# A planner that takes the longest-free buffer or PSUM bank instead of the lowest-numbered one, and a later due time for one transpose

## The chip, the core and the metric

The kernel runs on one core of one Trainium2 chip. A core has five engines with their own instruction queues: TensorE (PE, matrix multiplies and transposes into the eight PSUM banks), VectorE (DVE), ScalarE (ACT), GpSimd (POOL) and SyncE (SP, which here only issues DMAs). Each engine runs its queue in program order and waits on semaphores for the others. The metric is device time in microseconds, from the launch of the program to its end; lower is better.

## What is computed

Inputs are q, k, v of shape 2 x 8 x 768 x 64 (batch, heads, positions, head size) and four weight matrices. The reference is three steps:

```
state = gamma[head] * state + outer(k[t], v[t])      # per head, t = 0..767, gamma = 1 - 2**(-5-head)
y[t]  = 1/sqrt(64) * q[t] @ state                    # retention, a linear attention with decay
x  = softplus(y @ w_in)  @ w_out                     # y as 1536 x 512; w_in 512 x 2048, w_out 2048 x 512
out = hardswish(x @ w2_in) @ w2_out                  # hardswish(h) = h * clip(h + 3, 0, 6) / 6
```

The weights arrive as 64-bit floats and are read as pairs of 32-bit words.

## The kernel before

**Three kinds of work share the engines.** (1) Retention: 12 units, one for each batch and each chunk of 128 positions, in `attend(u)`. A unit loads k, q and v; transposes k and q on PE into PSUM; ACT copies kT out and DVE multiplies q by a scaling table into qT; PE computes scores; DVE masks them into `pt`; PE computes the state's increment (`product`: k with vs, the scaled v), the inner part (`inner`: pt with vs) and the carried part (`carry`: qT with the state `st`); ACT and DVE write the result as a high and a low part, `x_hi` and `x_lo`. (2) Weights: 64 tiles, each fetched as 64-bit words into `raw`, turned into float32 in `cv` by two ACT and three DVE instructions, and split into a high and a low part in `w` (the low part by DVE or by an adding DMA from POOL). (3) Two GEMM layers, `gemm1` and `gemm2`, 12 matmuls of 128 x 512 per step (high x high, high x low, low x high), 96 steps of `gemm1` and 96 of `gemm2`, with softplus or hardswish on ACT and DVE between them. The first four units of retention must be done before the first `gemm1`; the other eight are woven between GEMM steps.

**What sets the order.** The class `Plan` is a list scheduler that runs while the kernel is built. Each piece of work is a task with an engine, an estimated cost, the tasks it follows, a due time, and the slots that it takes and gives. `run` keeps an estimated clock for each engine, looks at the first 80 tasks of each, takes among those that can start within `NEAR` of the first (0.5 for PE) the one with the lowest due time, and issues its instructions at once. The order of those picks is the program order of every engine. The times in the planner are estimates made at build time; the chip only sees the order and which slot each task got.

**Slots.** A pool (`raw0`, `cv0`, `w`, `e`, `g`, `hi`, `lo`, `kT0`, `qT0`, `st`, ..., and `bank` for the eight PSUM banks) is a list of the estimated times from which each slot is free. `places` picks slots. It is called twice: without `at`, to learn when a task could start, and with `at`, the chosen start, to take slots. With `at` every slot free by then counted as equally free, so `sorted(..., key=(time, i))` took the lowest number and, for banks, `min` took the first group in the list of `bank_groups`. For units 0 to 3 that list is the pairs 2-3, 4-5, 6-7, 0-1 (or the single banks of these in that order); for later units only 2 and 3; `gemm1` alternates in 0 and 1, `gemm2` has 4 to 7. A slot taken again makes the first instruction that writes it wait, on the chip, for the last one that used it.

**The start of the program.** PE first runs 16 idle transposes, then `wide_turned`: four transposes that turn the scaling table (spread by DVE into an `e` tile) into PSUM under the key `tqP`. ACT copies that into `tq_sb`. Then come unit 0's transposes of k (`kP`) and of q (`qP`), 4 each. With the lowest number taken, `tqP`, `kP` and `qP` all sat in bank 2, one after another.

Of the kernel before, what the change touches and what calls it, by code (L numbers as in the profile page):

```python
# [22 lines left out]
class Plan:  # L23
# [37 lines left out]

    def places(self, pool, keys, at=None):

        times = {i: x if at is None else max(x, at) for i, x in enumerate(self.pools[pool]) if x is not None}
        if pool in self.groups:
            ok = [g for g in self.groups[pool](keys) if all(i in times for i in g)]
            return min(ok, key=lambda g: max(times[i] for i in g), default=None)
        return sorted(times, key=lambda i: (times[i], i))[:len(keys)] if len(times) >= len(keys) else None

    def run(self, log=None):  # L70
        free = {"PE": 0.0, "DVE": 0.0, "ACT": 0.0, "POOL": 0.0, "SP": 1.2}
        line = {"SP": 0.0, "POOL": 0.0}
        todo = {e: sorted((t for t in self.tasks if t.eng == e), key=lambda t: (t.due, t.n)) for e in free}
        left = {k: len(v) for k, v in self.users.items()}
        for _ in self.tasks:
            best = None
            for e, ts in todo.items():
                found = []
                for t in ts[:80]:
                    if any(a.done is None for a in t.after):  # L80
                        continue
                    at = max([free[e], t.hold] + [a.done + (self.LAG[a.eng] if a.eng != e else 0.0) for a in t.after])
                    for pool in {p for p, _ in t.take}:
                        ok = self.places(pool, [k for p, k in t.take if p == pool])
                        if ok is None:
                            break
                        at = max(at, max(self.pools[pool][i] for i in ok))
                    else:
                        found.append((at, t))
                if not found:  # L90
                    continue
                first = min(a for a, _ in found)
                at, t = min(((a, t) for a, t in found if a <= first + self.NEAR[e]), key=lambda x: (x[1].due, x[1].n))
                if best is None or at < best[0]:
                    best = at, t
            if best is None:
                raise RuntimeError("the plan is stuck: " + str([(e, ts[0].n, ts[0].take) for e, ts in todo.items() if ts]))
            at, t = best
            for pool in {p for p, _ in t.take}:
                keys = [k for p, k in t.take if p == pool]  # L100
                for key, i in zip(keys, self.places(pool, keys, at)):
                    self.pools[pool][i] = None
                    self.slot[key] = pool, i
            end = free[t.eng] = at + t.cost
            if t.load:
                other = "SP" if t.eng == "POOL" else "POOL"
                begin = max(line[t.eng], end + 1.2)
                shared = max(0.0, min(t.load, line[other] - begin))
                line[t.eng] = begin + t.load + shared
                line[other] += shared  # L110
                end = line[t.eng] + 0.5
            t.done = end
            for k in t.give:
                left[k] -= 1
                if not left[k]:
                    pool, i = self.slot[k]
                    self.pools[pool][i] = max(u.done for u in self.users[k])
            todo[t.eng].remove(t)
            if log is not None:
                log.append((at, end, t))  # L120
            t.fn()
# [7 lines left out]
def kernel(ctx, tc, q, k, v, w1_in, w1_out, w2_in, w2_out, table, out):  # L129
    nc = Plan(tc)  # L130
# [102 lines left out]
    due, t = {}, 5.0  # L233
# [158 lines left out]
    def bank(key):  # L392
        return at_slot(key).rearrange("p (n t) -> p n t", n=NP)
# [3 lines left out]
    def attend(u):  # L397
        b, i = divmod(u, NCH)
# [11 lines left out]
        def own(n):  # L410
            return [(f"{n}{ph}", (n, u))]
# [12 lines left out]
        if u < START:  # L424
            at = [begin + 10 * u, begin + 10 * u + 1, begin + 10 * u + 3]
        else:
            at = [d["Tk"] - 9.0, d["Tk"] - 8.5, d["Tk"] - 8.0]
# [4 lines left out]
        if u == 0:  # L432
            ready["t"] = nc.add("SP", 0.45, lambda: nc.sync.dma_start(out=tables, in_=table), [], begin - 1, load=0.1)
            t = nc.add("DVE", 0.62, spread_out, [ready["t"]], begin, take=[("e", "wide")])
            t = nc.add("PE", 0.46, wide_turned, [t], 0.0, take=[("bank", ("tqP", 0))], give=["wide"])
            ready["q"] = nc.add("ACT", ACP, lambda: nc.scalar.activation(tq_sb, bank(("tqP", 0)), AF.Copy), [t], begin, give=[("tqP", 0)])

        def turned(n):
            def go():
                for p in range(NP):  # L440
# [6 lines left out]
                  take=own("kT"), give=[("kP", u)])  # L447
# [29 lines left out]
        def middle():  # L477
            if first:
                nc.vector.tensor_copy(at_slot(mid[1]), sub(ds, 0))
            else:  # L480
# [3 lines left out]
                  give=ds + ([] if first else [("end", u - 1)]))  # L484
# [21 lines left out]
        def carry():  # L506
            for j in range(int(first), 2):
                w = at_slot(mid[1] if j else ("end", u - 1))
                for p in range(NP):
# [7 lines left out]
                 give=[mid[1], ("qT", u)] + ([] if first else [("end", u - 1)]))  # L517
# [10 lines left out]
    for u in range(NU):  # L528
        attend(u)
# [140 lines left out]
```

## Time and profile before

| | us |
|---|---|
| Median of 3 runs (lowest, highest) | 603.46 (602.60, 604.37) |
| Profiled execution, whole | 602.95 |
| its span, first to last instruction | 601.2 |
| around the span (602.95 - 601.2) | 1.75 |
| PE busy, of the span | 586.3 |
| PE not busy (601.2 - 586.3) | 14.9 |
| DVE busy, ACT busy | 326.4, 305.5 |

The profile is one execution. A row of the timeline gives the start and the length of an instruction or a run of like instructions, and in brackets how long its engine was idle before it and which engine's instruction released it. On PE a run of matmuls reads "start, length, output<-inputs, shape, count"; `ident,k` are the transposes of k, `qT,kT` the scores, `vs,k` the product, `pt,vs` the inner part, `qT,st` the carried part, `x_hi,w` a `gemm1`. The 64 x 64 matmuls show twice as many records as the program has instructions. A row of the windows view gives each engine's busy time within a stretch, then PEclk, the mean granted clock of TensorE as a share of full speed (its two levels are 1.2 and 2.4 GHz, 0.50 and 1.00).

### The profile page before, as it was taken

To read this page: it belongs to the slowest core of one execution; us is meant where nothing else is said; L and a number is where in the kernel's file an instruction comes from. 1 tells how busy PE (TensorE), PEld (TensorE's weight loads), DVE (VectorE), ACT (ScalarE), POOL (GpSimd) and SP (SyncE) were. 2 spreads that over 40 slices of the span, in tenths; PEclk is the share of its full clock that TensorE was granted. 3 is DMA by queue.
4 is the path that set the end of the run, shared out by engine and by line. 5 is a ranking of instruction groups with operands and counts; after the bars stand their busy time and mean duration, and the time that the engine had idled before them with its cause. 6 is when DMAs were issued, how large, how long until landed. Compare 5 with 4: busy or idle time off the path is not lost.

```text
span 601.2 us, 9628 instructions
## 1 busy us (share of the span) xinstructions
PE 586.3 (98%) x3895; PEld 479.1 (80%) x3895; DVE 326.4 (54%) x573; ACT 305.5 (51%) x515; POOL 40.3 (7%) x53
## 2 busy tenths in 40 slices
PE   7799999999999999999999999999999999999997
PEld 6678777878777788888888787888888888888886
DVE  3989999986544433566677876622422222412223
ACT  2469898895323333577789888622222222222220
POOL 0001111010000000011122222100000000000000
PEclk8789999999999999999999999999999999999999
DMA  9969887763111200065779988410100000100001
GB/s 198 243 159 228 223 219 191 203 148 71 41 31 37 71 1 0 1 151 130 179 181 225 224 207 200 98 19 0 71 0 1 1 1 0 71 0 1 1 0 70
DMA packets 67500, 58.56 MB, mean 97 GB/s; under 512 B 39552, under 2 KB 56192, under 8 KB 67456
## 3 DMA queue, kind: packets, MB, share of 16 engines
q1 hardware_dynamic: 60976, 46.15, 27.5%
q0 software_dynamic: 6480, 11.80, 11.3%
q8 instruction: 30, 0.49, 0.3%
q14 instruction: 14, 0.11, 0.1%
HBM read 43.00 MB, written 3.15 MB: 77 GB/s over the span
## 4 chain that ended last, share of the span: by engine, by line
PE 85%; DVE 4%; DMA 4%; ACT 4%; issue 1%; POOL 0%; DVEq 0%; SPq 0%; ACTq 0%; POOLq 0%
PE banks L42 85%; DMA raw<-in_moe_w_out_dram 4%; DVE cv L42 2%; ACT raw L42 1%; ACT w L42 1%; ACT cv L42 1%; ACT g L42 0%; ACT hi L42 0%; ACT e L42 0%; DVE raw L42 0%; DMA out_dram<-e 0%; DVE qT L42 0%; DVE g L42 0%; DVE pt L42 0%; DVE st L42 0%
## 5 line engine op out<-in xcount | busy, mean ns | idle before, releaser
L42 PE MATMUL banks<-x_hi,w 128*128 128x512 f32 x768 | 254.1, 393 | 2.0 <-DVE g L42 1.5
L42 PEld LDWEIGHTS banks<-x_hi,w 128*128 128x128 f32 x768 | 144.2, 188 | 34.0 <-DVE g L42 2.5
L42 PE MATMUL banks<-x_lo,w 128*128 128x512 f32 x384 | 149.6, 390 | 0.0
L42 PE MATMUL banks<-hi,w 128*128 128x512 f32 x384 | 127.8, 395 | 0.0
L42 PE MATMUL banks<-w,hi 128*128 128x512 f32 (+1 forms) x386 | 118.3, 388 | 0.0
L42 ACT ACTIVATE e<-banks,three 128x512 f32<-128x512 f32 x48 | 33.0, 686 | 128.2 <-PE banks L42 120.7
L42 DVE SCALAR_TENSOR_TENSOR g<-e,banks 128x512 f32<-128x512 f32 x48 | 33.0, 688 | 115.5 <-ACT e L42 115.1
L42 DVE TENSOR_TENSOR lo<-g,hi 128x512 fp32r<-128x512 f32 x96 | 66.1, 690 | 48.7 <-ACT hi L42 45.6
L42 DVE SCALAR_TENSOR_TENSOR cv<-raw,cv 128x512 uint32<-128x512 uint32 x128 | 87.5, 689 | 8.1 <-ACT cv L42 5.5
L42 ACT ACTIVATE hi<-g 128x512 fp32r<-128x512 f32 x96 | 60.5, 630 | 51.9 <-DVE g L42 36.3
L42 PEld LDWEIGHTS banks<-hi,w 128*128 128x128 f32 x384 | 72.1, 188 | 15.6
L42 PEld LDWEIGHTS banks<-w,hi 128*128 128x128 f32 x386 | 72.4, 188 | 14.9
L42 PEld LDWEIGHTS banks<-x_lo,w 128*128 128x128 f32 x384 | 72.1, 188 | 14.3
L42 PE MATMUL banks<-w,lo 128*128 128x512 f32 (+1 forms) x193 | 74.9, 388 | 0.0
L42 PE MATMUL banks<-lo,w 128*128 128x512 f32 x192 | 74.9, 390 | 0.0
L42 ACT ACTIVATE w<-cv 128x512 fp32r<-128x512 f32 x109 | 65.5, 624 | 8.0 <-DVE cv L42 7.6
L42 POOL DMA_DIRECT2D w<-cv x45 | 39.2, 872 | 349.4 <-ACT w L42 203.6
L42 ACT ACTIVATE g<-banks 128x512 f32<-128x512 f32 x48 | 28.6, 595 | 53.6 <-PE banks L42 51.1
L42 ACT ACTIVATE cv<-raw,half 128x512 uint32<-128x512 uint32 x64 | 48.2, 758 | 0.0
L42 ACT ACTIVATE raw<-raw 128x512 f32<-128x512 f32 x64 | 42.8, 668 | 3.6 <-DMA raw<-in_moe_w_out_dram 3.4
L42 PEld LDWEIGHTS banks<-w,lo 128*128 128x128 f32 x193 | 36.2, 188 | 7.5
L42 PEld LDWEIGHTS banks<-lo,w 128*128 128x128 f32 x192 | 36.1, 188 | 7.0
(58 smaller groups left out, 325.2 us busy)
## 6 DMA issues: line engine op xcount, KB each, us to landing
raw<-in_moe_w_in_dram SPq DMA_DIRECT2D x32, 512.0 KB, 4.1
raw<-in_moe_w_out_dram SPq DMA_DIRECT2D x32, 512.0 KB, 3.6
w<-cv POOLq DMA_DIRECT2D x45, 256.0 KB, 4.6
out_dram<-e SPq DMA_DIRECT2D x11, 256.0 KB, 2.0
q<-in_q_dram SPq DMA_DIRECT2D x8, 256.0 KB, 5.2
v<-in_v_dram SPq DMA_DIRECT2D x8, 256.0 KB, 5.4
k<-in_k_dram SPq DMA_DIRECT2D x7, 256.0 KB, 4.8
raw<-in_k_dram SPq DMA_DIRECT2D x4, 256.0 KB, 3.1
```

Of the source, the lines that this page charges most:

```text
L42: return self.plan.tc.keep_in_program_order(getattr(self.engine, op)(*args, **kwargs))
```

## The change

`places` keeps, for each free slot, the pair (time from which the task could have it, time since which it is free). Where several slots are free by `at`, the first entries are equal and the second decides: the one longest free is taken, in every pool and for bank groups alike. In `run` the start of a candidate is now the maximum over the slots' free times as before, written without the pair. The due time of `wide_turned` goes from 0.0 to 5.2, between unit 0's k (due 5.0) and q (5.46).

```diff
     def places(self, pool, keys, at=None):
 
-        times = {i: x if at is None else max(x, at) for i, x in enumerate(self.pools[pool]) if x is not None}
+        free = {i: x for i, x in enumerate(self.pools[pool]) if x is not None}
+        times = {i: (x if at is None else max(x, at), x) for i, x in free.items()}
         if pool in self.groups:
             ok = [g for g in self.groups[pool](keys) if all(i in times for i in g)]
             return min(ok, key=lambda g: max(times[i] for i in g), default=None)
@@ run
-                        at = max(at, max(self.pools[pool][i] for i in ok))
+                        at = max([at] + [self.pools[pool][i] for i in ok])
@@ attend, unit 0
-            t = nc.add("PE", 0.46, wide_turned, [t], 0.0, take=[("bank", ("tqP", 0))], give=["wide"])
+            t = nc.add("PE", 0.46, wide_turned, [t], 5.2, take=[("bank", ("tqP", 0))], give=["wide"])
```

The program order, first place: PE at the start of the program, from the turned scaling table (`ident,e`) to unit 0's scores (`qT0,kT0`). Rows with a minus are of before, with a plus of the changed kernel; the brackets name the semaphores waited on (`Activation` is ACT, `DMAHW` a load).

```order
 L42 MATMUL banks_65<-ident_139,e_0_103 128x128 x3
-L42 MATMUL banks_65<-ident_139,k0_0_123 128x128 [waits DMAHW1_49,Activation_49]
+L42 MATMUL banks_65<-ident_139,k0_0_123 128x128 [waits DMAHW1_49]
 L42 MATMUL banks_65<-ident_139,k0_0_123 128x128
 L42 MATMUL banks_65<-ident_139,k0_0_123 128x128 [waits DMAHW2_49]
-L42 MATMUL banks_65<-ident_139,q0_0_120 128x128 [waits DMAHW3_49,Activation_49]
+L42 MATMUL banks_65<-ident_139,q0_0_120 128x128 [waits DMAHW3_49]
 L42 MATMUL banks_65<-ident_139,q0_0_120 128x128 x3
-L42 MATMUL banks_65<-qT0_0_130,kT0_0_129 64x64 [waits DVE_49]
+L42 MATMUL banks_65<-qT0_0_130,kT0_0_129 64x64 [waits DVE_49,Activation_49]
```

The order of the rows is unchanged: the table's transposes still stand ahead of k's. What moved is the waits: k and q no longer wait for ACT, since the three take banks 2, 3 and 4; the scores now name ACT themselves, for kT. With the new due time alone the program is that of before row for row on all five engines, and with the new `places` alone it is the changed one.

Second place: PE from unit 3's transposes of k to unit 4's transposes of q, the last retention work but one ahead of the first `gemm1`. `k0_0` and the first `pt` are unit 3's, `k0_1` and `q0_1` unit 4's. First the kernel before, then the changed one.

```order
L42 MATMUL banks_65<-ident_139,k0_0_123 128x128 [waits DMAHW0_49,DVE_49]
L42 MATMUL banks_65<-vs0_0_132,k0_0_123 64x64 [waits DVE_49]
L42 MATMUL banks_65<-qT0_0_130,kT0_0_129 64x64 [waits Activation_49]
L42 MATMUL banks_65<-pt0_0_134,vs0_0_132 64x64 [waits DVE_49]
L42 MATMUL banks_65<-ident_139,k0_1_124 128x128 [waits DMAHW1_49,DVE_49]
L42 MATMUL banks_65<-ident_139,q0_1_121 128x128 [waits DMAHW2_49]
```

```order
L42 MATMUL banks_65<-ident_139,k0_0_123 128x128 [waits DMAHW0_49]
L42 MATMUL banks_65<-vs0_1_133,k0_0_123 64x64 [waits DVE_49]
L42 MATMUL banks_65<-qT0_1_131,kT0_0_129 64x64 [waits Activation_49]
L42 MATMUL banks_65<-ident_139,k0_1_124 128x128 [waits DMAHW1_49,DVE_49]
L42 MATMUL banks_65<-pt0_1_135,vs0_1_133 64x64 [waits DVE_49]
L42 MATMUL banks_65<-ident_139,q0_1_121 128x128 [waits DMAHW2_49]
```

Unit 4's transposes of k moved ahead of unit 3's inner part, and unit 3's transposes of k lost their wait for DVE.

Third place: PE among the GEMM steps, around the transposes of unit 5 (`k_0`, `q_0` before; `k_2`, `q_2` now). `x_hi_66,w_83` ends a `gemm1`, `hi_...,w_85` is a `gemm2`. First before, then changed.

```order
L42 MATMUL banks<-x_hi_66,w_83 128x512
L42 MATMUL banks<-hi_107,w_85 128x512
...
L42 MATMUL banks<-ident,k_0_123 128x128 x4
L42 MATMUL banks<-ident,q_0_120 128x128 x4
L42 MATMUL banks<-x_hi_66,w_84 128x512
...
L42 MATMUL banks<-qT_0_130,kT_0_129 64x64 x16
```

```order
L42 MATMUL banks<-x_hi_66,w_83 128x512
L42 MATMUL banks<-ident,k_2_125 128x128 x4
L42 MATMUL banks<-ident,q_2_122 128x128 x4
L42 MATMUL banks<-hi_108,w_85 128x512
...
L42 MATMUL banks<-qT_1_131,kT_0_129 64x64 x16
L42 MATMUL banks<-x_hi_66,w_84 128x512
```

From here to the end of unit 7 every retention piece stands one GEMM step earlier in PE's queue; DVE's and ACT's queues shift with it between their weight and softplus instructions. Behind that the orders of before and now are the same on every engine but for slot numbers.

## Rows read from the trace of the kernel before

**Rows 1.** Page, part 1: engine, busy us, share of the span, instructions

```profile
PE 586.3 (98%) x3895; PEld 479.1 (80%) x3895; DVE 326.4 (54%) x573; ACT 305.5 (51%) x515; POOL 40.3 (7%) x53
```

**Rows 2.** Windows: stretch, its us, busy us (instructions) of five engines, PEclk, DMA share, GB/s

```profile
6.50:10.00 3.50, 1.78 (x36) 1.31 (x40) 1.22 (x2) 0.72 (x2) 0.00 (x0) 0.99 1.26 222
10.00:13.40 3.40, 3.40 (x85) 2.83 (x78) 2.04 (x5) 0.60 (x1) 0.00 (x0) 0.51 1.32 221
13.40:23.60 10.20, 7.91 (x278) 6.73 (x280) 9.13 (x21) 5.10 (x9) 0.00 (x0) 1.00 1.02 262
23.60:33.80 10.20, 8.07 (x133) 6.58 (x130) 8.86 (x17) 3.84 (x8) 0.00 (x0) 0.50 0.59 161
33.80:37.00 3.20, 2.37 (x96) 2.12 (x93) 3.04 (x6) 2.78 (x5) 0.00 (x0) 1.00 1.24 291
```

**Rows 3.** Timeline of PE, 0 to 38 us

```profile
4.92 1.06 PE L42 MATMUL banks<-ident,e 128*128 128x128 f32 x4
6.67 0.66 PE L42 MATMUL banks<-ident,k 128*128 128x128 f32 x4 [0.69 <-ACT tq_sb L42]
8.02 0.66 PE L42 MATMUL banks<-ident,q 128*128 128x128 f32 x4 [0.69 <-ACT kT L42]
9.53 0.84 PE L42 MATMUL banks<-qT,kT 64*64 64x64 f32 x32 [0.85 <-DVE qT L42]
10.14 1.12 PE L42 MATMUL banks<-vs,k 64*64 64x64 f32 x32
...
13.30 0.66 PE L42 MATMUL banks<-ident,q 128*128 128x128 f32 x4
...
15.34 0.69 PE L42 MATMUL banks<-vs,k 64*64 64x64 f32 x32
...
17.33 0.66 PE L42 MATMUL banks<-ident,q 128*128 128x128 f32 x4
...
21.38 0.69 PE L42 MATMUL banks<-pt,vs 64*64 64x64 f32 x32 [1.24 <-DVE st L42]
...
24.10 1.11 PE L42 MATMUL banks<-ident,q 128*128 128x128 f32 x4
...
30.38 1.13 PE L42 MATMUL banks<-pt,vs 64*64 64x64 f32 x32 [1.29 <-DVE pt L42]
31.44 1.11 PE L42 MATMUL banks<-ident,k 128*128 128x128 f32 x4
32.34 1.06 PE L42 MATMUL banks<-ident,q 128*128 128x128 f32 x4
...
36.61 0.50 PE L42 MATMUL banks<-x_hi,w 128*128 128x512 f32 x1
```

**Rows 4.** Windows: one unit's stretch; the GEMM steps beside the weights

```profile
13.95:18.05 4.10, 3.78 (x123) 3.05 (x124) 3.78 (x8) 1.19 (x2) 0.00 (x0) 1.00 1.10 346
40.00:122.00 82.00, 81.53 (x730) 64.52 (x729) 77.06 (x148) 70.35 (x123) 8.83 (x10) 1.00 0.79 209
```

**Rows 5.** Timeline of PE, 100 to 125 us

```profile
121.33 0.50 PE L42 MATMUL banks<-x_hi,w 128*128 128x512 f32 x1 [0.47 <-ACT g L42]
```

**Rows 6.** Timeline of SP: issues of q and v of unit 0, q of unit 3

```profile
2.18 0.51 SPq L42 DMA_DIRECT2D q<-in_q_dram  x1
2.74 0.58 SPq L42 DMA_DIRECT2D v<-in_v_dram  x1
...
12.62 0.49 SPq L42 DMA_DIRECT2D q<-in_q_dram  x1
```

**Rows 7.** DMA issues from 1 to 3.3 us: KB each, median us to landing

```profile
q<-in_q_dram SPq DMA_DIRECT2D x1, 256.0 KB, 3.4
v<-in_v_dram SPq DMA_DIRECT2D x1, 256.0 KB, 4.1
```

**Rows 8.** Timeline of DVE, 0 to 38 us

```profile
33.44 0.69 DVE L42 TENSOR_TENSOR qT<-banks,tq_sb 128x512 f32<-128x512 f32 x1 [1.11 <-PE banks L42]
```

**Rows 9.** DMA issues from 12.6 to 22.7 us

```profile
q<-in_q_dram SPq DMA_DIRECT2D x2, 256.0 KB, 6.7
```

## The prediction

> **What bounds the kernel now.** I read the page first: PE is busy 586.3 of 601.2 us [rows 1], and nearly all of that is GEMM steps, which the change neither adds nor removes. So only PE's 14.9 idle us and its clock can move. Then the windows view, to see where they lie [rows 2]. From 6.5 to 37 us the five stretches last 30.5 us with PE busy 1.78 + 3.40 + 7.91 + 8.07 + 2.37 = 23.53: 6.97 idle us, nearly half of all. In two of these stretches PE runs at the lower clock, 10.0 to 13.4 (0.51) and 23.6 to 33.8 (0.50). Then PE's timeline of the start [rows 3], whose brackets name who ends each idle piece. From 40 to 122 us PE is busy 81.53 of 82.00 [rows 4]; the 0.47 left is one wait for ACT at 121.33 [rows 5]. DVE is busy 77.06 of those 82, 94%. So the start is a chain PE-ACT-PE-DVE-PE; from 13.4 on DVE carries it (9.13 and 8.86 of 10.2 busy [rows 2]); behind the first GEMM step at 36.61 PE is the bound and DVE close behind it.
>
> **The due time.** It removes, adds and moves nothing: with it alone every engine's order is that of before, since the table is ready so much ahead of k's load that the planner picks it first either way. Price 0. All that follows is the choice of slots.
>
> **Unit 0: two bank waits go.** Before, the table's transposes (4.92, 1.06 long, to 5.98), k's and q's share a bank: k starts 0.69 late, released by the copy to tq_sb, q 0.69 late, released by the copy to kT; the scores start 0.85 behind q's end (8.68 to 9.53), which is qT's multiply [rows 3]. With three banks k and q follow at once, if loaded: q is issued at 2.18 and v at 2.74 [rows 6] and land 3.4 and 4.1 later [rows 7], at 5.6 and 6.8; k is issued ahead of q. Four transposes take 0.66 here, but the table's took 1.06, the pace of the lower clock (1.06 and 1.11 stand again at 32.34 and 31.44, where PEclk is 0.50). The clock rose somewhere between 5.98 and 6.67, so k now falls across the rise: I take the mean, 0.86, for k and 0.66 for q. Then q ends at 5.98 + 0.86 + 0.66 = 7.50 and the scores start 0.85 later, 8.35 instead of 9.53: 1.2 gained. Bounds: both slow, 5.98 + 2.12 + 0.85 = 8.95, 0.6; both fast, 8.15, 1.4. The scores' new wait for ACT costs nothing: kT is ready 0.69 behind k's end, at 7.5, ahead of qT, and only the product stands behind the scores, which needs vs, made on DVE behind qT as before.
>
> **The clock behind it.** Ahead of the slow stretch at 10.0 PE was idle 3.50 - 1.78 = 1.72 us; in 33.8 to 37.0 it was idle 0.83 and the clock stayed at 1.00 [rows 2]. Without the two waits what is left in front is the 0.85, like the second case, so I expect the clock to stay up through 10.0 to 13.4. Worth: product, k, inner part up to the next q take 10.14 to 13.30, 3.16 us, at 0.51, and 15.34 to 17.33, 1.99, at 1.00: 1.17 at most. DVE has 2.04 us of its own in that stretch, which then fill it, so I take 0.9, between 0 (the clock falls all the same) and 1.2.
>
> **Units 2 and 3: waits that cost nothing.** The inner part at 21.38 waited 1.24 for DVE's state additions, which free its bank pair; it now has an older pair and waits only for its mask. Unit 3's k likewise no longer waits for the bank that its q left. I count both at 0: DVE is full there, and what PE does next waits for DVE's queue anyway. If DVE had room there, the first could give up to 1.24.
>
> **Unit 4's k ahead of unit 3's inner part.** PE idled 1.29 before that inner part, for the mask. k's transposes now fill this gap, so q's come one transpose step earlier, 32.34 - 31.44 = 0.90; DVE idled 1.11 for them at 33.44 [rows 8]. k still waits for DVE; if that wait ends as late as the mask, nothing is gained: 0 to 0.9. Behind qT DVE has weight work of its own ahead of unit 4's mask, so I take 0.5.
>
> **Does it last?** The start is moved by 1.2 + 0.9 + 0.5 = 2.6. It would be lost if loads bound it. They are issued as before: unit 3's q at 12.62 [rows 6], 6.7 to land [rows 9], is there at 19.3, and is used at 24.10: 4.8 in hand. The raw weights are fetched again when DVE frees their buffers, so they move along. Units 5 to 7 stand one GEMM step earlier in the queues; their work leaves DVE a step sooner, which relieves it ahead of the wait at 121.33. Of that 0.47 I take 0.2, between -0.5 (as much lost in a new wait) and 0.47. Behind 122 us the orders are the same, and what is left there stays.
>
> **Sum.** 1.2 + 0.9 + 0.5 + 0.2 = 2.8. The profiled execution of before took 602.95 as a whole (span 601.2 and 1.75 around it), so 600.15 against its own time. The median shown is 603.46, 0.5 above that execution; against it, 603.46 - 2.8 = 600.7.
>
> **Rivals.**
> *The clock takes part of it back.* The stretch at 10.0 stays slow (no 0.9), and the later slow stretch, 10.2 us long before, ends after the first GEMM step instead of 2.8 us ahead of it. For it: this step comes earlier, and PE still idles in front. Against: the gaps are shorter. If a slow piece as long as that of 10.0 to 13.4 fell on GEMM steps it would cost half of 3.4, 1.7. So 1.2 + 0.5 + 0.2 = 1.9 less 0 to 1.7, in the middle 1.05 gained: 602.4. One variant has a page behind it: the Trainium skill, "TensorE: Matmul & The Clock Gate", section "A second HAM failure mode: psum-queue depth-cycling", tells of a kernel that cycled through PSUM banks and idled so often between groups that its clock went up and down. By that rule rotating banks would itself bring slow stretches into the GEMM steps. The trace speaks against it: the two `gemm1` banks alternate before too, and 40 to 122 us has PEclk 1.00 [rows 4]. The same page, "What's actually happening", says that where the clock rises at the start differs from run to run; no row here shows that, and the terms above do not use it.
>
> *DVE gives it back.* PE starts its steps earlier, but weights come no sooner, and PE waits somewhere in 40 to 122. For it: DVE at 94%. Against: DVE's own start moves too, since its first multiply waits for q's transposes. Some 0.3 would be left: 603.2.
>
> *Slower.* Units 5 to 7 stand one step earlier among the GEMM steps, so their DVE work comes ahead of weights that are due. One unit has 3.78 us of it (13.95 to 18.05 [rows 4]); DVE's idle time, 82.00 - 77.06 = 4.94, is 1.2 for each of the four units there (4 to 7). Where a weight has no slack PE then waits 3.78 - 1.2 = 2.6. One such wait leaves the time as before; from two on it is slower: 603.46 - 2.8 + 5.2 = 605.9. Against: PE waits for a weight nowhere in that stretch before, so there is slack, though its size can't be read.
>
> **Chances and range.** Forecast 0.64, clock 0.20, DVE 0.10, slower 0.06. About 0.3%, 1.8 us, is what a measurement of this kernel can tell from no change: 601.65 and 605.27. Past 601.65 lie nearly all of the forecast (0.60) and two fifths of the clock case (0.08): faster 0.68; slower is most of the last case, 0.05; within, 0.27. The ends of the terms add to 0.1 and 4.0, but seldom all at once: for the forecast alone 1.5 to 4.1 gained (599.4 to 602.0). The range goes on past the middle of the clock case: 599.4 to 602.7.
>
> **What would show it.** k's and q's transposes directly behind the table's, the scores near 8.35; no stretch at 0.5 near 10 to 13; no wait of unit 2's inner part for `st`, and yet no gain there; unit 4's k between unit 3's scores and its inner part; the first `x_hi,w` near 34.0; PE still full from there to 122, and the same length from there to the end but for 121.33. I am wrong if the first GEMM step moves by less than 1.5, or if it moves and PE then waits for `w` or `g` before 122.

## The result, and the profile after

The changed kernel takes 596.78 us (median of 4 runs, 596.09 to 598.96) against 603.41 (602.60 to 604.37) for the kernel before: a ratio of 0.9896, with a 95% interval of 0.9866 to 0.9925. The forecast was 600.7, its range 599.4 to 602.7: right that it gets faster, but the gain is 6.6 us where 2.8 was forecast. The profiled execution of the changed kernel took 596.94 as a whole, 595.2 in its span, 6.0 less than the 601.2 of before. Of one experiment, `g2`, the profiled execution was disturbed, so that only its times are used.

First the page, part 1 and the chain of waits by engine, of the changed kernel.

```profile
PE 582.8 (98%) x3895; PEld 477.6 (80%) x3895; DVE 326.2 (55%) x573; ACT 304.9 (51%) x515; POOL 40.3 (7%) x53
...
PE 96%; DVE 2%; issue 1%; DMA 0%; POOL 0%; DVEq 0%; POOLq 0%
```

Against [rows 1] PE is busy 3.5 us less (less of it at the lower clock) and idle 12.4 instead of 14.9. The windows view of the same stretches as [rows 2, 4], and two more:

```profile
6.50:10.00 3.50, 2.64 (x103) 2.37 (x104) 3.04 (x6) 0.76 (x2) 0.00 (x0) 1.00 1.29 221
10.00:13.40 3.40, 3.07 (x94) 2.38 (x92) 3.08 (x8) 0.88 (x2) 0.00 (x0) 1.00 1.13 194
13.40:23.60 10.20, 6.56 (x194) 5.67 (x194) 7.69 (x17) 5.96 (x10) 0.00 (x0) 0.92 0.92 240
23.60:33.80 10.20, 8.21 (x207) 6.56 (x206) 10.06 (x20) 5.32 (x9) 0.00 (x0) 0.74 0.86 242
...
40.00:122.00 82.00, 82.00 (x733) 65.23 (x732) 77.71 (x147) 72.00 (x127) 9.85 (x12) 1.00 0.80 207
122.00:335.00 213.00, 213.00 (x1385) 173.46 (x1384) 123.21 (x218) 123.34 (x213) 18.06 (x21) 1.00 0.40 96
335.00:365.00 30.00, 30.00 (x134) 24.83 (x133) 22.94 (x40) 27.66 (x51) 7.69 (x9) 1.00 0.94 231
```

The stretch at 10.0 runs at full clock now (0.51 before), the next low one is shorter, and 40 to 122 us, 82.00 of 82.00, has lost its wait. What I had not read before is the same view of the kernel before, further on:

```profile
122.00:335.00 213.00, 213.00 (x1385) 173.36 (x1384) 123.43 (x218) 123.58 (x214) 18.25 (x21) 1.00 0.39 92
335.00:369.00 34.00, 32.49 (x142) 26.05 (x141) 25.74 (x45) 30.23 (x54) 7.82 (x9) 1.00 0.88 212
```

From 335 to 369 us, 1.51 us of PE were idle before; the changed kernel has no idle time there at all. Its start, PE's timeline to the first `gemm1`, answers to [rows 3]:

```profile
4.93 0.61 PE L42 MATMUL banks<-ident,e 128*128 128x128 f32 x4
5.38 0.60 PE L42 MATMUL banks<-ident,k 128*128 128x128 f32 x4
5.81 0.60 PE L42 MATMUL banks<-ident,q 128*128 128x128 f32 x4
7.36 0.69 PE L42 MATMUL banks<-qT,kT 64*64 64x64 f32 x32 [0.94 <-DVE qT L42]
...
9.70 0.66 PE L42 MATMUL banks<-ident,q 128*128 128x128 f32 x4
...
14.35 0.66 PE L42 MATMUL banks<-ident,q 128*128 128x128 f32 x4
...
17.38 0.27 PE L42 MATMUL banks<-pt,vs 64*64 64x64 f32 x1 [0.30 <-DVE pt L42]
20.37 0.69 PE L42 MATMUL banks<-pt,vs 64*64 64x64 f32 x31 [2.73 <-issue]
21.34 1.44 PE L42 MATMUL banks<-qT,st 64*64 64x64 f32 x32 [0.27 <-DVE seen L42]
22.71 1.11 PE L42 MATMUL banks<-ident,q 128*128 128x128 f32 x4
24.86 1.12 PE L42 MATMUL banks<-ident,k 128*128 128x128 f32 x4 [1.04 <-DMA k<-in_k_dram]
...
27.83 1.11 PE L42 MATMUL banks<-ident,k 128*128 128x128 f32 x4
28.93 0.69 PE L42 MATMUL banks<-pt,vs 64*64 64x64 f32 x32
29.55 0.66 PE L42 MATMUL banks<-ident,q 128*128 128x128 f32 x4
...
33.61 0.50 PE L42 MATMUL banks<-x_hi,w 128*128 128x512 f32 x1
```

Start against start, the lead over before is 2.17 us at unit 0's scores (9.53 to 7.36), 3.60 at unit 1's q (13.30 to 9.70), 2.98 at unit 2's q (17.33 to 14.35), only 1.01 at unit 2's inner part (21.38 to 20.37), 1.39 at unit 3's q, 2.79 at unit 4's q and 3.00 at the first `gemm1`. From there PE never stops. The chain of waits of the changed kernel (start, length, what) has the whole of the GEMMs as one piece:

```profile
17.65 2.73 issue
32.98 555.46 PE banks L42 x3292
589.19 2.02 DMA out_dram<-e
```

The other 3.0 us of the span come behind the first `gemm1`, at three places. One is 121.33, known from [rows 5]. The others are in PE's waits of the kernel before (for what, us in all, times, longest), a view of which I had read only the part up to 122 us:

```profile
PE banks L42 <- DVE g L42: 1.5, 2, 0.8
```

The second of these two, with the instructions around it on PE and DVE, in the kernel before and then in the changed one:

```profile
361.71 0.39 PE L42 MATMUL banks<-w,lo 128*128 128x512 f32 x1
...
362.20 0.69 DVE L42 SCALAR_TENSOR_TENSOR g<-e,banks 128x512 f32<-128x512 f32 x1
...
362.94 0.50 PE L42 MATMUL banks<-x_hi,w 128*128 128x512 f32 x1 [0.85 <-DVE g L42]
```

```profile
356.70 0.69 DVE L42 SCALAR_TENSOR_TENSOR g<-e,banks 128x512 f32<-128x512 f32 x1
356.84 0.39 PE L42 MATMUL banks<-w,lo 128*128 128x512 f32 x1
357.07 0.39 PE L42 MATMUL banks<-x_hi,w 128*128 128x512 f32 x1
```

Before, `g` (hardswish's last product, which reads the PSUM bank of the `gemm1` ahead) ends at 362.89 and the next `gemm1` starts 0.05 later: it writes the same bank. In the changed kernel the same `gemm1` starts at 357.07 while `g` runs to 357.39: it writes the other bank. By the planner's slots, the kernel before put 89 of its 96 `gemm1` steps in bank 0 and 7 in bank 1; the changed one takes 0 and 1 in turn, but for one step. From `w,lo` to `x_hi` the wait cost 1.23 - 0.23 = 1.00 us, more than the 0.85 in the bracket. The lead at these places: 3.00 at the first `gemm1`, 3.78 behind 121 us (a `hi,w` at 309.17 before, 305.39 now), 4.60 at the next (339.91 to 335.31), 5.87 at 362.94 to 357.07.

### The profile page after: what moved, and what is told of

Read it like the earlier page. It is cut to its first block, busy times and chain, and to the rows that moved or that the text cites. A ratio compares the mean times of both kernels' runs of the same rounds, so it can differ in the third digit from the quotient of the medians.

```text
span 595.2 us, 9589 instructions
## 1 busy us (share of the span) xinstructions
PE 582.8 (98%) x3895; PEld 477.6 (80%) x3895; DVE 326.2 (55%) x573; ACT 304.9 (51%) x515; POOL 40.3 (7%) x53
## 4 chain that ended last, share of the span: by engine, by line
PE 96%; DVE 2%; issue 1%; DMA 0%; POOL 0%; DVEq 0%; POOLq 0%
PE banks L42 96%; DVE cv L42 0%; DVE qT L42 0%; DVE pt L42 0%; DMA out_dram<-e 0%; DVE w L42 0%; DVE vs L42 0%; DVE x_lo L42 0%; DVE e L42 0%; DVE raw L42 0%; DVE st L42 0%; DVEq L667 0%; POOL ident masks.py:199 0%; POOL e masks.py:65 0%; DVE seen L42 0%
```

## Experiments

All are edits of the changed kernel. A kernel that has the new rule for some slots alone has this in `places`, and only `longest` is given below:

```diff
-        times = {i: (x if at is None else max(x, at), x) for i, x in free.items()}
+        longest = ...
+        times = {i: (x if at is None else max(x, at), x if longest else 0.0) for i, x in free.items()}
```

"Start" is the first `gemm1` of its profiled execution, "body" the span from there to the end (before: 36.61 and 564.59; changed: 33.61 and 561.59). The body is the steadier of the two: a second profile of the changed kernel has 35.02 and 561.58.

**Which slots carry the gain (four kernels, beside before at 603.79).**

```diff
+        longest = not (pool == "bank" and keys[0][0] == "h")     # e1_h_lowest: all but gemm1's banks
+        longest = pool == "bank" and keys[0][0] == "h"           # e2_h_only: gemm1's banks alone
+        longest = pool == "bank" and keys[0][0] != "h"           # e3_ret_banks_only: retention's banks alone
+        longest = pool != "bank"                                 # e4_buffers_only: SBUF buffers alone
```

> The changed kernel, but the banks of gemm1 (h) are taken lowest number first, as before, so nearly every gemm1 writes bank 0; all other pools take the longest free. Program order is that of the changed kernel. Bank theory (PE waited at 121.33, 339.91 and 362.94 us of before because one h bank had to be emptied before the next gemm1): some of these waits come back, 0.5 to 3 us longer than the changed kernel, 597.3 to 599.8, and PE rows released by ACT g or DVE g stand in the profile. Buffer theory (weights come sooner because raw, cv, w, e, g, hi and lo rotate, and so the waits go): no waits, 596.8.

Measured 598.74, ratio 0.9916 (0.9896 to 0.9937), start 33.9, body 564.1. The waits for `g` are back; DVE and PE of this kernel:

```profile
347.16 0.68 DVE L42 SCALAR_TENSOR_TENSOR g<-e,banks 128x512 f32<-128x512 f32 x1
...
347.89 0.50 PE L42 MATMUL banks<-x_hi,w 128*128 128x512 f32 x1 [0.44 <-DVE g L42]
```

> The kernel before, but with the longest-free rule for the h banks of gemm1 alone, so they alternate in 0 and 1; order as before. Bank theory: the three waits of PE go, 0.5 to 0.8 us at 121 and 1.5 to 2.25 at 340 to 363, so 600.4 to 601.4, with the start unchanged (first gemm1 near 36.6 us). Buffer theory: no change, 603.4.

Measured 600.26, ratio 0.9946 (0.9927 to 0.9966), start 37.38, body 562.82. The program order is that of before and no wait for DVE's `g` is left, but the one near 121 us, for ACT's, is still there; PE's timeline of this kernel:

```profile
122.66 0.50 PE L42 MATMUL banks<-x_hi,w 128*128 128x512 f32 x1 [1.01 <-ACT g L42]
```

So two causes are apart. The waits at 340 and 363 us are bank 0 taken twice running: in all seven profiles with the old rule for `gemm1`'s banks one or more of these steps starts late, in none of the eight with the new rule. The wait at 121 us is not (the banks alternate there in the kernel before too); it goes with the moved order. In the seven profiles that keep the order of before, this `gemm1` starts 0.47 to 1.40 us behind the matmul ahead of it, where 0.23 is the step without a wait; in the others at most 0.42 (`e1`).

> The kernel before, but with the longest-free rule for the retention's banks alone (tables, k, q, scores, increments, outputs); h banks and all buffers lowest number first. Program order is that of the changed kernel. Start theory: the first gemm1 comes about 2.9 us sooner than before, as in the changed kernel, and the time is 600.5; the waits for g at 340 to 363 stay. If the start's gain needed the rotated buffers too, 602 to 603.4.

Measured 600.46, ratio 0.9948 (0.9927 to 0.9968), start 33.56, body 563.64, the order of the changed kernel but for slots and 9 rows of SP. About half of the gain is here, most of it in the start.

> The kernel before, but with the longest-free rule for every pool of buffers and lowest number first for all banks; order as before but for a few swaps of loads. Bank and start theory: no change, 603.4 within 0.6. Buffer theory: the weights come sooner, PE's waits for DVE g at 340 to 363 go, 600.5 to 601.5.

Measured 602.75, ratio 0.998 (0.9964 to 0.9995), start 37.39, body 563.71: the buffers give about 1 us (1.2, 0.3 to 2.2, by the ratio; 0.88 in the body of its profile), and nothing in the start. The prediction had no term for them.

**Unit 0's banks, the ACT pools, the loads, all banks (beside before at 602.53).** `f1` and `f2` set `longest`, `f3` is the changed kernel with one weight tile fetched ahead of unit 3's loads, not three.

```diff
+        longest = pool == "bank" and keys[0] in (("tqP", 0), ("kP", 0), ("qP", 0))     # f1_unit0_banks
+        longest = pool in ("e", "g", "hi", "lo")                                       # f2_act_pools
-    AHEAD = 3
+    AHEAD = 1                                                                          # f3_ahead1
+        longest = pool == "bank"                                                       # f4_banks_only
```

> The kernel before, with the longest-free rule for unit 0's three transposes alone (table, k, q in three banks); every other slot and the whole order as before. If the two waits at the start are worth what they cost on TensorE (2.1 us by the changed kernel's scores at 7.36 against 9.53, and 1.4 more where the clock then stays up behind them) and this reaches the first gemm1: 600.3 to 601.7. If VectorE's later queue (full from 14 to 32 us) or the loads swallow it: 603 to 603.6. In the changed kernel about half of the first lead of 3.5 us was lost again at 17 to 25 us, so I expect the middle, 601.7 to 602.5.

Measured 601.37, ratio 0.9979 (0.9962 to 0.9996): 1.3 us (0.2 to 2.3), start 35.27, body 564.13, the order of before. PE's timeline of this kernel:

```profile
4.93 1.06 PE L42 MATMUL banks<-ident,e 128*128 128x128 f32 x4
5.79 0.77 PE L42 MATMUL banks<-ident,k 128*128 128x128 f32 x4
6.39 0.60 PE L42 MATMUL banks<-ident,q 128*128 128x128 f32 x4
7.94 0.69 PE L42 MATMUL banks<-qT,kT 64*64 64x64 f32 x32 [0.94 <-DVE qT L42]
...
29.01 0.69 PE L42 MATMUL banks<-pt,vs 64*64 64x64 f32 x32 [2.23 <-DVE pt L42]
29.63 0.79 PE L42 MATMUL banks<-ident,k 128*128 128x128 f32 x4
30.22 1.06 PE L42 MATMUL banks<-ident,q 128*128 128x128 f32 x4
```

The scores come 1.59 earlier than before, but unit 3's inner part only 1.37 (30.38 to 29.01), and it waits 2.23 for its mask. In the changed kernel unit 4's k stands in that gap.

> The kernel before, with the longest-free rule for e, g, hi and lo alone (the buffers between the two GEMMs); raw, cv, w and all banks as before. Rotating all buffers gave -1.0 us (ratio 0.998, 0.9964 to 0.9995). If that came from e and g, whose reuse held back the instruction that empties gemm1's bank: 602.5 to 603. If it came from the weights' buffers: 603.4 to 604.

Measured 601.63, ratio 0.9992 (0.9975 to 1.0009): no change, though its body is 562.61 in the profile. There the `gemm1` steps sit in the same banks as before, and yet of the waits for `g` only 0.23 us are left, at 359.78. So rotating these buffers can shorten the same waits as another bank does. But the profiled execution, 599.77, is the fastest of the twelve, and the times show no gain of 2 us; how large the waits are differs between executions.

> The changed kernel with AHEAD = 1: only one weight tile is loaded ahead of unit 3's q, v and k, not three. In the changed kernel PE waited 1.04 us for unit 3's k, landed at 24.9. Load theory (that load now bounds the start): k lands about 3 us sooner, that wait goes, the first gemm1 comes about 1 us sooner, near 32.6, and the time is 595.6 to 596.3. If VectorE's queue or the code loading (PE idle 2.73 us at 17.65 with no releaser) bounds it: 596.8, no change. If the two weight tiles that now come later hold up the first GEMM steps: 597.5 to 599.

Measured 600.91, ratio 0.9974 (0.9958 to 0.999), slower than the changed kernel: the start is 33.14, but the body 567.56. Between 36 and 62 us ACT waits 1.7 and 1.0 us for loads of `raw`, where it waits for none in the changed kernel; DVE, which works on what ACT has turned, comes late, and PE waits for it among the GEMM steps:

```profile
62.03 0.68 PE L42 MATMUL banks<-vs,k 64*64 64x64 f32 x16 [2.24 <-DVE pt L42]
```

> The kernel before, with the longest-free rule for all PSUM banks (retention and gemm1) and lowest number first for every buffer. Bank theory: nearly the whole gain, 596.8 to 597.5. If the buffers add what they gave alone: 597.6 to 598.2.

Measured 598.03, ratio 0.994 (0.992 to 0.996), start 36.77 in a profile whose lower clock lasts from 20.8 to 34.5, body 562.03, no PE gap behind the first `gemm1`. The time lies in the second range, so the buffers add to the banks. Against `e3`, whose planner orders and slots are the same up to the first `gemm1`, the body is 1.61 shorter and the time 0.5 us (0.9948 and 0.994).

**Whole and parts once more (beside before at 602.26).** `g2` and `g4` set `longest`, `g3` has `AHEAD = 2`.

```diff
+        longest = pool == "bank" and (keys[0] in (("tqP", 0), ("kP", 0), ("qP", 0)) or keys[0][0] == "h")            # g2
+        longest = pool == "bank" and keys[0][0] != "h" and keys[0] not in (("tqP", 0), ("kP", 0), ("qP", 0))        # g4
```

> The changed kernel once more, beside the three below on the same chip, so that parts and whole share one reference. Both theories: about 6.6 us less than before (0.989), no half-clock stretch at 10 us, no PE gap behind the first gemm1 step.

Measured 596.96, ratio 0.991 (0.989 to 0.9929): 5.4 us, within the interval of the first comparison.

> Longest-free only for unit 0's three banks and for gemm1's h banks; the program order is that of before. Theory (the gain is the earlier start plus the h banks that alternate): f1's 1.2 and e2's 3.3 add, 4.5 or more, so 599 or less, PE without a gap from the first gemm1 on, and the rest up to the whole change is the moved order (unit 4's k). Rival (one of the two hides the other, so that most of the gain needs the later units' banks): about e2's 3.3 alone, 600.2.

Measured 599.44, ratio 0.9954 (0.9937 to 0.997). The sum of parts is missed: 2.8 us, not 4.5. `h2` below goes on from there.

> Longest-free only for the retention banks of everything but unit 0's tqP, kP and qP; the program order is that of before. The prediction's term for units 2 and 3 was 0, since DVE is full there: then the time is before's within 1 us, although unit 2's inner part no longer waits 1.24 for st. Rival (that wait was on the path): 1.2 less, with the first gemm1 step that much earlier.

Measured 603.96, ratio 1.0027 (1.0015 to 1.004): slightly slower, 1.6 us (0.9 to 2.4), which neither theory had. That the wait for `st` is worth nothing by itself stands; why the kernel is slower is open. Its profile differs from before's from the first transposes on: k's take 1.12, not 0.66, and the inner part at 13.41 still 1.11, the pace of the lower clock, so that the scores start at 10.45 and not 9.53. Whether the other executions do so too, no run shows.

> The changed kernel with two weight tiles instead of three fetched ahead of unit 3's loads (the order of some PE pieces moves with it). Theory: the changed kernel's wait of 1.04 us for unit 4's k goes, since loads are less crowded, and the start gains up to 1; with one tile PE later waited 2.24 us for a weight, with two half as much or nothing: 596 to 598. Rival: a weight comes late as with one tile, 599 to 601.

Measured 597.35, ratio 0.9915 (0.9897 to 0.9933): the same as the changed kernel. (The wait of 1.04 us named above is that of unit 3's k, not unit 4's.) The start is earlier, 31.89, and the body longer, 565.11: PE waits 1.78 for `pt`, and then the clock falls among the GEMM steps. Timeline and windows of this kernel:

```profile
56.95 0.68 PE L42 MATMUL banks<-vs,k 64*64 64x64 f32 x16 [1.78 <-DVE pt L42]
```

```profile
58.60:62.00 3.40, 3.40 (x9) 2.30 (x7) 2.50 (x5) 3.00 (x6) 0.00 (x0) 0.51 0.94 243
```

**Unit 4's k held back, and `g2` with a profile (beside before at 602.35).**

```diff
-        tp = task("PE", cost["Tk"], turned("k"), [ik, ready.get(("o", u - 1)) if u > START else None], d["Tk"], take=[("bank", ("kP", u))])
+        tp = task("PE", cost["Tk"], turned("k"), [ik, ready.get(("o", u - 1)) if u > START else ready.get("I") if u == START else None], d["Tk"], take=[("bank", ("kP", u))])
...
         n = task("PE", cost["I"], inner, [pt, vs], d["I"], take=[("bank", x) for x in o], give=[("pt", u), ("vs", u)])
+        ready["I"] = n
```

> The changed kernel, with unit 4's transposes of k held behind unit 3's inner part, where they stood before (the planner then also puts unit 4's scores and product behind the first gemm1 steps, as work moved, not saved). Theory (the start's gain beyond unit 0's banks, about 1.9 by all retention banks against unit 0's alone, is this move): 1.9 more than the changed kernel, 598.7. Rival (it is the later units' banks, or unit 0's gain that lasts): the changed kernel's time within 0.6. The term on record for the move was 0.5, which would be 597.3 and can't be told from the rival.

Measured 602.09, ratio 0.9986 (0.9963 to 1.0009): nearly the whole gain is gone, more than either theory had. Timeline and windows of this kernel:

```profile
28.97 0.69 PE L42 MATMUL banks<-pt,vs 64*64 64x64 f32 x32 [2.56 <-DVE pt L42]
30.24 1.91 PE L42 MATMUL banks<-qT,st 64*64 64x64 f32 x32 [0.57 <-DVE seen L42]
33.56 1.11 PE L42 MATMUL banks<-ident,k 128*128 128x128 f32 x4 [1.42 <-DVE x_lo L42]
```

```profile
30.40:37.20 6.80, 5.38 (x45) 4.81 (x44) 5.41 (x11) 5.76 (x10) 0.00 (x0) 0.50 0.86 198
```

PE stops 2.56 and 1.42 in place of working on unit 4, and the lower clock behind that reaches past the first `gemm1`, 35.18 here. As the planner also moved unit 4's scores and product, and work behind them on other engines, the 5 us are not the price of the one move. That the move is worth more than the 0.5 on record fits them, but is not shown by a run that changes so much besides.

> Unit 0's banks and the h banks again, for a profile that can be read (the first one's execution was disturbed). Its time came out 2.8 under before, not the 4.5 that the parts added to. Theory A (the parts do not add because the earlier start is used up between unit 0 and the first gemm1): first gemm1 near 36.5 as before, body near 562. Theory B (they add but the h banks alone are worth less than e2's 3.3, whose start happened to be early): first gemm1 near 35.5, body 562 to 562.5, time 599.5.

Measured 599.11, ratio 0.9952 (0.9933 to 0.9971), start 34.74, body 562.56: theory B. The start is 1.87 earlier than before's and the body 2.03 shorter, so both parts are there. Of `e2`'s 3.3 us its own body explains 564.59 - 562.82 = 1.77; its order and slots up to the first `gemm1` are before's and its profiled start is no earlier, so the rest is probably the spread between executions and not the h banks. What the changed kernel has beyond `h2` (0.9896 and 0.991 against 0.9952, 2.5 to 3.4 us) is the moved order and the other slots.

## Why the prediction was wrong, point by point

**What failed** is the step "Behind 122 us the orders are the same, and what is left there stays". The orders are the same; the slots are not, and a PSUM bank that is taken again is a wait. The two waits for `g`, 1.51 us by their brackets, cost 0.82 (from 4.60 - 3.78) and about 1.0 plus small ones, 2.2 together in the profile, and were taken as 0. The page of before held them. PE's idle time was 14.9, and the views that I used account for 6.97 + 0.47 = 7.44 of it; I never asked where the other half lay (1.97 ahead of 6.5 us, 1.51 in these waits, 4.00 behind 369 us, nearly all of it behind the last matmul). Of the signs named in advance, the one that failed outright is "the same length from there to the end". The clock rival and the description of the kernel say that `gemm1` alternates between two banks before the change: that is wrong, read from the list of allowed banks in the code. The old rule took bank 0 whenever it was free. `e1` (waits back) and `e2` (waits gone, order as before) show the cause.

The size of this step is less sure than 2.2. In seven profiles with the old banks the late steps from 335 to 364 us lose 0.2 to 1.8 us, and before's is the largest. The four pairs that differ in `gemm1`'s banks alone (before and `e2`, `f1` and `h2`, `e3` and `f4`, `e1` and the changed kernel) differ by 1.57 to 2.51 in the body and by 0.4 to 3.3 in the time. The sum also left out the buffers, worth about 1 us in `e4`.

**The due time: 0, right.** **Unit 0's waits: 1.2, right in kind, too small.** k and q follow the table's transposes directly. In the changed kernel the scores lead by 2.17, since the table's transposes already took 0.61, which is the higher clock; with the slower start of `f1` it is 1.59, past my bound of 1.4. I added lengths of 1.06, 0.86 and 0.66, but runs on PE overlap: in `f1` they start 0.86 and 0.60 apart, and the scores at 7.94, not 8.35. `f1`'s time, 1.3 (0.2 to 2.3), holds this term and the next, 2.1 by forecast.

**The clock behind it: 0.9, right in kind.** 10.0 to 13.4 has PEclk 1.00, and the lead grows by 1.43 to unit 1's q, past my top of 1.2. The clock falls between 8.4 and 10.0 us in three of the five profiles with the old banks of unit 0 (before, `e2`, `e4`), and in none of the ten with the new ones before 19 us. It does not fall there in `f2`, so part of this term may be the one execution of before that I read.

**Units 2 and 3: 0, right by luck.** The wait for `st` went, and PE then stopped 2.73 at the same inner part with nothing in the trace that it waited for (the last section has more on this). The lead fell from 2.98 to 1.01, a loss that no term had. I had DVE as what comes next; but DVE's `seen` waits for PE there. Nor did I foresee that unit 3's k would now wait 1.04 for its load; q's issue is at 14.31 in the changed kernel (12.62 in [rows 6]), so the loads were not "issued as before".

**Unit 4's k: 0.5, too small.** From unit 3's inner part to unit 4's q the lead grows from 1.45 to 2.79, by 1.34, past my bound of 0.9: besides k's 0.90, which now fills the gap of [rows 3], the inner part runs at full clock, 0.69 for 1.13, because the low stretch now ends ahead of it. DVE's wait in [rows 8] is gone too:

```profile
30.65 0.69 DVE L42 TENSOR_TENSOR qT<-banks,tq_sb 128x512 f32<-128x512 f32 x1
```

So the start comes out at 3.00 against 2.6, by errors that cancel and in one execution of each kernel. **The wait at 121.33: 0.2, and the lead grew by 0.78 there**: all of the wait went, and a bracket of 0.47 stood for 0.86 - 0.23 = 0.63 between two matmuls' starts (120.47 and 121.33 before, against 0.23 within a step). The sum, in the two profiles: 3.00 + 0.78 + 2.2 = 6.0 where 2.6 + 0.2 + 0 = 2.8 was forecast.

**The rivals.** None of them decided. PE does wait 1.78 and 2.24 for DVE's work in `g3` and `f3`, as in "DVE gives it back", but these two fetch weight tiles later by their edit; with the loads of the changed kernel and its start of 33.61 there is no such wait. The clock among GEMM steps is what `g3` shows at 58.6. The page that I weighed against the change, the Trainium skill, "TensorE: Matmul & The Clock Gate", section "A second HAM failure mode: psum-queue depth-cycling", tells of a kernel that cycled through banks, idled between its groups and so went slow again and again. Here two banks in turn left no idle time between the steps, and PEclk is 1.00 from 40 to 365 us. The rule that I passed over is in the Trainium skill, "Perfetto Trace Analysis", section "Matmuls": independent groups of matmuls should rotate through PSUM banks, so that emptying one overlaps the next group. The trace agrees: the two steps of 96 that had waited 0.66 and 0.85 for `g` no longer wait.

**Still open:** what stops PE for 2.73 us; why the later units' banks alone cost 1.6; how the start's gain beyond unit 0 splits between moved order and later banks. By the times of kernels that each add to the one before, unit 0's banks gave 1.3 (`f1`), the other retention banks with the moved order 1.9 more (`e3`), `gemm1`'s banks 0.5 more (`f4`), and the buffers 1.8 to 2.6 more (the changed kernel); each step is uncertain by about 1 us, and the parts depend on the order in which they are added.

## What to carry to other kernels

Account for all idle time of the bounding engine before pricing a change: list every wait over the whole span, and let a term be 0 only where the list is empty. A change of which buffer is taken is a change of waits wherever that pool is used, even where the order stays; read from the built program which slot each step got, not from the slots that it may have. Price a wait by the interval between the two starts, not by its bracket alone. Read a term of the start from several executions.

## What the runs showed of the hardware

PE can stop without a wait. In the changed kernel, its second profile, `e1`, `e3`, `f3`, `f4`, `g3` and `h1` the same inner part of unit 2 stands still for 2.73, 2.45, 2.3, 1.8, 1.5, 3.3, 1.8 and 2.0 us, marked "issue". DMA issues and queues from 13 to 22 us in the changed kernel show full DMA engines, and packets of instructions among them:

```profile
q1 hardware_dynamic: 3855, 2.14, 88.7%
q8 instruction: 2, 0.03, 1.7%
```

The packets of q8 hold 16 KB each; the trace has their times. In all fifteen profiles that can be read, unit 2's inner part starts or goes on 1.2 to 1.6 us behind the landing of the second such packet of the span, whatever the bracket names. In the changed kernel this packet starts at 17.89 and lands at 18.90, and PE goes on at 20.37; in the kernel before, at 20.01 and 21.38, where the bracket names `st`, which ends at 21.35. In `f1`, where it lands at 18.56, the bracket names a `cv`, although `st` ended at 18.36:

```profile
19.93 1.14 PE L42 MATMUL banks<-pt,vs 64*64 64x64 f32 x32 [2.79 <-DVE cv L42]
```

So the stop does not need the moved order, which `f1` has not, and it would explain why a lead of 2.98 us shrinks to 1.01 there: the packet lands only 1.11 sooner. That PE waits for code, which comes behind the loads, fits all fifteen, but no edit moved a packet by itself, so it is not shown.

Where the lower clock falls differs between executions of one program. The second profile of the changed kernel has it from 19.0 to 32.7 us, all at half speed, and its first `gemm1` at 35.02, not 33.61, with the same body:

```profile
19.00:32.70 13.70, 11.52 (x199) 9.77 (x200) 11.09 (x23) 5.73 (x10) 0.00 (x0) 0.50 0.81 195
```

So a term of the start, read from one execution, can be off by 1.4 us here, while the two bodies agree within 0.01. Between kernels whose orders and slots are the same up to the first `gemm1` it is more: 33.56 in `e3` and 36.77 in `f4`, with the lower clock from 20.5 to 23.9 and from 20.8 to 34.5, and 36.61, 37.38 and 35.39 in before, `e2` and `f2`. The mean of these three against that of the changed kernel's 33.61 and 35.02 and `e1`'s 33.90 gives a lead of 2.3, not 3.00.
